# Cache loads of the last two steps on GpSimd's DMA queue, in a decode kernel whose order is computed by a scheduler

## The chip, the core and the metric

The kernel runs on one core of a Trainium2 chip. The metric is device time in microseconds (us) of one execution. The core has five instruction streams that matter here: TensorE (PE), VectorE (DVE), ScalarE (ACT), GpSimd (POOL) and SyncE (SP). Each runs its own instructions strictly in the order in which the program lists them. SP does nothing but issue DMA transfers; GpSimd computes and issues DMAs too. The transfers that SP issues go into one DMA queue (q1 in the profile), those of GpSimd into another (q0). Both queues are served by the same 16 DMA engines.

## What is computed

A forward pass and all its gradients, for two batch rows of one token each (decode), everything in bf16:

```python
xn  = layernorm(x)                         # x: [2, 1, 576]
q   = xn @ wq                              # 32 query heads of 128, 16 cache heads
p   = softmax(q . k_cache * 128**-0.5)     # k_cache, v_cache: [2, 16, 4096, 128]
out = x + (p @ v_cache) @ wo + ((xn @ w_gate) * (xn @ w_up)) @ w_down
# outputs: out, and the gradients for grad_out of
# x, k_cache, v_cache, wq, wo, w_gate, w_up, w_down
```

The caches hold 32 MB each, and their gradients have the same size. So 64 MB of cache are read and 64 MB of cache gradient are written; the weights (wq, wo, w_gate, w_up, w_down) add about 25 MB in each direction. The gradients are outer products: the gradient of V for a head is p (4096 long) times the incoming gradient (128 long), that of K is the score gradient times q.

## The kernel before

**Steps.** The work on the caches is cut into 16 steps (`NS`), numbered s = 0 to 15. A step handles two cache heads (l = 0, 1) of one batch row; two steps (the two batch rows) make a group, and there are 8 groups. In a step, t = 0 stands for K and t = 1 for V. Each (s, t, l) is one tile of 128 partitions x 8192 bytes, 1 MB, loaded whole by one DMA: 4 loads in a step, 64 in all. They are issued in `load_kv` (the DMA is on line 986).

**What a step does.** `turn` transposes each loaded tile on DVE in two halves (line 411). `softmax` multiplies the transposed K by the queries (`score`, 64 small matmuls, line 1096), takes the softmax and spreads the probabilities into the layout that the next matmuls want (`spread`, lines 1103 and 1104, through the tile `sp`, then a DVE transpose into `pp`). `dscore` does the same for V with the incoming gradient, and gets the score gradient, which it spreads through the same tile `sp` into `dd`. `contract` multiplies the untransposed tile by `pp` or `dd` (line 1272); only after that is the 1 MB buffer of the load free (`free_kv`). `outer` and `head_outer` make the gradient of the cache: matmuls against `BD`, a block-diagonal tile that GpSimd builds (line 1084, 4 in a group, one per step and t), two PSUM banks at a time, copied to a 1 MB buffer by ACT (line 415) or DVE (line 417), four copies for one buffer. The full buffer is stored by one DMA of SP (line 642, in `put`). There are 64 such stores of 1 MB.

**Weights.** Each group has a `group_front` (queries, loads of wq and wo) and a `group_back` (gradients of wq and wo). Nine blocks of the gated MLP (`mlp`) are sprinkled over the steps. The loads of wq, wo, w_gate and w_up and the stores of all weight gradients (0.5 and 0.56 MB, and tails of 64 KB) are issued by GpSimd; w_down is loaded by SP. After the last group, `final_out` and `final_dx` write out the two small results `out` and the gradient of x.

**Buffers.** Sixteen buffers of 1 MB (`big`) are shared by three users: loaded cache tiles (`kv`), transposed tiles (`X`) and stores being filled or in flight (`st`). `CAP` says how many each user may hold at once.

**Who sets the order.** The program has no order of its own. Every piece of work is a Python generator that yields requests (`ACQ` a buffer, `WAIT` for an event, occupy an engine for so long, issue a `DMA`), and the class `Order` runs them all in a simulated time before the chip sees anything. For each engine it takes, among the requests that can start within `SLACK` us of the earliest one, that with the lowest priority number, and the instructions are emitted in that order. Priorities are `PR[name] + STEP * s`, with corrections in `HEAD` for the first two steps and `TAIL` for the last two. `CAP`, `BIAS` (how readily a PSUM copy goes to DVE instead of ACT), `MLPD` (distance of MLP blocks, in cache loads) and `WO0` shift the order too. On the chip, semaphores guard every dependency: a wrong guess of the order costs waiting.

Two consequences matter. SP's list holds cache loads and cache stores mixed: a load stands behind every store that precedes it in the list, first on SP (which waits until that store's data is ready) and then in the DMA queue. And GpSimd's list holds `BD` builds, small copies and DMA issues mixed, with the same rule.

Of the kernel before, what the change touches and what calls it, by code (L numbers as in the profile page):

```python
# [95 lines left out]
class Order:  # L96

    HOP, TAIL, DRAIN = 0.07, 0.18, {"PE": 0.0, "ACT": 0.1, "DVE": 0.075, "POOL": 0.0}

# [84 lines left out]
    def run(self):  # L184
        while self.streams:
# [8 lines left out]
            if e is not None:  # L194
                t, _, s, e = min((c for c in cand if c[3] == e and c[0] <= t + SLACK[e]), key=lambda c: (c[1], c[0]))
            r = s.req
            value = None
            if r[0] in ("op", "any"):
                cost = r[2] if r[0] == "op" else next(c for x, c, _ in r[1] if x == e)
                quad = r[3] if len(r) > 3 else None  # L200
                if e == "PE":
                    end = t + cost + self.TAIL
                    if quad is not None and self.quad[:2] == (1 - quad, t):
                        cost, end = 0.02, max(t + self.TAIL, self.quad[2]) + 0.02
                    self.quad, self.kind = (quad, t + cost, end), r[6]
# [29 lines left out]
def PE(stream, issue=0.0, quad=None, kind="f"):  # L235
    return ("op", "PE", max(CLK * stream, issue) + 0.03, quad, stream, issue, kind)


def DVE(cost):
    return ("op", "DVE", cost)  # L240
# [10 lines left out]
def EV(cols):  # L251
    return ("any", [("ACT", 0.16 + cols * 0.00083, 0.0), ("DVE", 0.145 + cols * 0.00104, cols / 1024 * BIAS)])


def ACQ(tag):
    return ("acq", tag)


def REL(tag, i):
    return ("rel", tag, i)  # L260


def WAIT(*events):
    return ("wait", events)


def SET(event):
    return ("set", event)


def SPAWN(gen, prio):
    return ("spawn", gen, prio)


def PRIO(prio):
    return ("prio", prio)


def DMA(engine, cost, nbytes, row=8192):
    packet = 0.0375 * row + 9.0  # L280
    return ("dma", engine, cost, 0.08 + nbytes / 16e3 * packet / row, packet)
# [1 line left out]


NBIG, NGU, NWW, NBD = 16, 1, 5, 3
CAP = {"kv": 8, "X": 14, "st": 12}
MLP0, MLPD = 0, 7.5
KVSTORE = "SP"
WQ0, WO0 = 0, 0
LATENCY, DRY = {"SP": 0.5, "ACT": 0.5, "POOL": 0.57}, 0.4  # L290
CLK = 2.0
BIAS = 0.63
SLACK = {"PE": 0.09, "ACT": 0.09, "DVE": 0.4, "POOL": 17.41, "SP": 26.84}
STEP = 28.0
HEAD = {"turn0": 3.0, "turn1": -11.1, "att": -19.9, "dsc": -4.3, "con": -39.4, "conv": -28.9, "out1": 42.9, "out0": 22.1, "front": -45.5, "back": 29.8, "W1": 86.9, "BD1": -12.5, "BD0": -10.4, "load": -8.1}
TAIL = {"turn0": 28.4, "turn1": 45.6, "att": 15.9, "dsc": -167.2, "con": -11.9, "conv": -61.9, "out1": -25.1, "out0": 3.1, "front": 0.8, "back": -31.6, "BD1": -11.1, "BD0": -158.9, "load": -37.4}
PR = {"turn0": -37.7, "turn1": 50.3, "att": -846.2, "dsc": -882.4, "conv": 130.3, "con": -283.8, "out1": 415.4, "out0": 232.2,
      "front": 147.9, "back": -713.6, "W0": 247.3, "W1": 250.7, "BD1": 345.9, "BD0": -138.7, "mlp": -163.6, "wout": -835.0,
      "store": 1037.0, "load": -22.4, "wload": -455.4, "fin": 234.1, "const": 420.2, "mload": 222.9}


def pr(name, s):
    edge = {} if type(s) is not int else HEAD if s < 2 else TAIL if s > 13 else {}
    return STEP * s + PR[name] + edge.get(name, 0)


@with_exitstack
def kernel(
# [22 lines left out]
    nc = tc.nc  # L331
# [7 lines left out]
    G = 2  # L339
    GH = 2 * G  # L340
    NG = Hkv // G
    NS = NG * Bq
# [12 lines left out]
    const = ctx.enter_context(tc.tile_pool(name="const", bufs=1))  # L355
# [4 lines left out]
    def tiles(tag, n, shape, dtype=BF16):  # L360
        od.ring(tag, n)
        return [const.tile(list(shape), dtype, name=f"{tag}{i}") for i in range(n)]

    kv_t = X_t = st_t = tiles("big", NBIG, [P, NCH * Dh])
    od.share("big", CAP)
    Xt_t = tiles("Xt", 1, [P, FS])
# [46 lines left out]
    def cp(e, out, in_):  # L413
        if e == "ACT":
            nc.scalar.copy(out, in_)  # L415
        else:
            nc.vector.tensor_copy(out=out, in_=in_)  # L417
# [100 lines left out]
    def front():  # L518
# [57 lines left out]

        yield PRIO(PR["const"])
        yield WAIT(Econst)
# [50 lines left out]
    class Store:  # L629
# [3 lines left out]
        def done(self):  # L633
            self.n -= 1
            if self.n == 0:
                yield SPAWN(self.out(), self.prio + PR["store"])

# [45 lines left out]
    def rows_outer(lhs, dst, p, events=()):  # L683
        i = yield ACQ("st")
        st = st_t[i]
        src = st[:, 0:FC * D].rearrange("p (h n) -> p h n", h=FC)
        store = Store(FC, put("POOL", [(dst, src, 128 * FC * D * 2)], "st", i, events, 4608), p)
        for a in range(FC):
            yield SPAWN(unit(*rows_unit(a, lhs, st), store), p)
# [35 lines left out]
    def mlp(i, Lgu, Ld, gs_slot, wd_slot):  # L725
# [41 lines left out]
        E = [Event() for _ in range(4)]  # L767
        po = pr("mlp", (MLP0 + i * MLPD) / 4) + PR["wout"]
        yield SPAWN(rows_outer(lambda a: hb[32 * a:32 * a + 32, 0, :],
# [125 lines left out]
    def group_back(g):  # L895
# [15 lines left out]
        E = [Event() for _ in range(3)]  # L911
        po = pr("back", 2 * g) + PR["wout"]
        yield SPAWN(rows_outer(lambda a: R[32 * a:32 * a + 32, 0, :],
# [60 lines left out]
    views = [A.rearrange("b h (p c) d -> b h p (c d)", p=P) for A in (A_k_cache, A_v_cache)]  # L974
    oviews = [A.rearrange("b h (p c) d -> b h p (c d)", p=P) for A in (out_2, out_3)]

    def load_kv():
        n = 0
        for s in range(NS):
            g, b = divmod(s, Bq)  # L980
            yield PRIO(pr("load", s))
            for t in range(2):
                for l in range(G):
                    i = yield ACQ("kv")
                    yield DMA("SP", 0.36, 1 << 20)
                    nc.sync.dma_start(kv_t[i][:], views[t][b, G * g + l])
                    kvS[s][t][l] = i
                    yield ("lset", kvL[s][t][l])
                    yield SET(issued[n])
                    n += 1  # L990
# [99 lines left out]
    def score(t, s, sc, l):  # L1090
        X = X_t[xS[s][t][l]]
        W = W_t[t][wS[s][t]]
        for be in range(4):
            for c2 in range(2):
                for cq in range(4):
                    nc.tensor.matmul(  # L1096
                        sc[32 * cq:32 * cq + 32, :],
                        lhsT=view(W[:], 0, P, (be * G + l) * WW + 6 - 4 * c2 - 2 * l, [[1, 32]]),
                        rhs=view(X[:], 0, P, (2 * cq + c2) * Dh + 64 * (be // 2) + be % 2, [[8 * Dh, 4], [2, 32]]),
                        start=(l == 0 and be == 0 and c2 == 0), stop=(l == G - 1 and be == 3 and c2 == 1))  # L1100

    def spread(src, dst_ps):
        nc.tensor.matmul(dst_ps[:, 0:P], lhsT=identP[:], rhs=src[:], start=True, stop=True)
        nc.tensor.matmul(dst_ps[:, P:2 * P], lhsT=src[:], rhs=identP[:], start=True, stop=True)
# [100 lines left out]
    def dscore(s):  # L1205
        S = steps[s]
        yield WAIT(wE[s][1], S["sm"], *xE[s][1])
        k = yield ACQ("m")
        dp = m_t[k][:, 0:P]
        for l in range(G):  # L1210
            yield PE(0.427, 0.224, kind="c")
            score(1, s, dp, l)
            yield REL("X", xS[s][1][l])
        yield REL("W1", wS[s][1])
        c = ch_t[S["ch"]]
        yield DVE(0.35)
        nc.vector.tensor_tensor_reduce(
            out=c["ds"][:], in0=c["ex"][:], in1=dp, scale=1.0, scalar=0.0,
            op0=ALU.mult, op1=ALU.add, accum_out=c["cs"][:],
        )  # L1220
        m = yield ACQ("m")
        yield PE(0.0, 0.1)
        nc.tensor.matmul(m_t[m][:, 0:1], lhsT=G4[:].rearrange("p a m -> p (a m)"), rhs=c["cs"][:], start=True, stop=True)
        yield DVE(0.15)
        nc.vector.tensor_tensor(c["cr"][:], m_t[m][:, 0:1], c["rz"][:], ALU.mult)  # L1225
        yield REL("m", m)
        yield DVE(0.3)
        nc.vector.scalar_tensor_tensor(out=c["ds"][:], in0=dp, scalar=c["cr"][:], in1=c["pr"][:],
                                       op0=ALU.subtract, op1=ALU.mult)
        yield REL("m", k)  # L1230
        S["dd"] = yield ACQ("dd")
        m = yield ACQ("m")
        yield PE(0.107, 0.052)
        spread(c["ds"], m_t[m])
        e = yield EV(256)
        cp(e, c["sp"][:], m_t[m][:, 0:2 * P])
        yield REL("m", m)
        yield DVE(0.4)
        t32(dd_t[S["dd"]][:].rearrange("p t n -> p (t n)"), c["sp"][:])
        yield REL("ch", S["ch"])  # L1240
        yield SPAWN(outer(s, 0, "dd", S["dd"], dd_t[S["dd"]][:, 1]), pr("out0", s))
        S["ddT"] = dd_t[S["dd"]][:]
        yield SPAWN(contract(s, 0), pr("con", s))
# [80 lines left out]
    def final_out():  # L1324
        yield PRIO(PR["fin"])
        yield WAIT(Eprep, *acc_E)
# [104 lines left out]
```

## Time and profile before

| | |
|---|---|
| median of 6 runs | 483.54 us (482.64 to 486.23) |
| profiled execution | 483.57 us, of which the span of the profile is 481.8 us |
| DMA | 185.94 MB, mean 386 GB/s; q1 (SP) 139.61 MB, q0 (GpSimd) 45.38 MB |
| busy, share of the span | PE 77%, DVE 72%, ACT 72%, GpSimd 51% |

How to read it: the span runs from the first to the last instruction of the profiled execution; the other 1.8 us lie around it. The page divides the span into 40 slices of about 12 us and gives for each the busy tenths of every engine, the mean busy share of the 16 DMA engines, and the GB/s that they moved. A list of waits names, for each engine and line, what it waited for. SPq is SP's queue of DMA issues. For a DMA, the profile tells when it was issued and when its last byte had landed.

### The profile page before, as it was taken

The numbers are of one execution on the slowest core, as the hardware profiler recorded it, in microseconds if no ns is written. First come the engines' busy times: TensorE is split into PE (matmuls) and PEld (weight loads), VectorE is DVE, ScalarE is ACT, GpSimd is POOL, SyncE is SP. The second block draws the span as 40 slices with busy tenths as digits, with TensorE's granted clock in tenths as the row PEclk, the third lists the DMA queues.
The fourth block names the chain that finished last, engine by engine and source line by source line (L and its number), as shares of the span: only waits on it lengthen the run. The fifth ranks groups of instructions, "written<-read, shape, count | busy, mean of one in ns | idle before, by whom it ended". The sixth has DMA issues, their size and how long they took to land.

```text
span 481.8 us, 14592 instructions
## 1 busy us (share of the span) xinstructions
PE 369.4 (77%) x6122; PEld 210.3 (44%) x6122; DVE 348.1 (72%) x662; ACT 346.1 (72%) x525; POOL 244.5 (51%) x348
## 2 busy tenths in 40 slices
PE   0578779664788589859776888887798878788886
PEld 0444445433454253435543543644454344434334
DVE  6798655883979465679887886887687775779763
ACT  6078847564889378917978589777867965878992
POOL 6185702772559126536384665272573756155501
PEclk9986765566786655565787577656656665857775
DMA  8999999899889999999999999999999999999995
GB/s 305 387 407 383 404 405 387 304 356 417 325 312 381 395 419 421 411 408 396 367 384 361 419 363 420 402 412 409 424 413 398 411 422 417 409 409 420 373 378 201
DMA packets 33445, 185.94 MB, mean 386 GB/s; under 512 B 5034, under 2 KB 5170, under 8 KB 16994
## 3 DMA queue, kind: packets, MB, share of 16 engines
q1 hardware_dynamic: 19866, 139.61, 72.1%
q0 software_dynamic: 13504, 45.38, 25.1%
q8 instruction: 48, 0.79, 0.6%
q14 instruction: 19, 0.16, 0.1%
q10 hardware_dynamic: 8, 0.00, 0.0%
HBM read 92.48 MB, written 92.48 MB: 384 GB/s over the span
## 4 chain that ended last, share of the span: by engine, by line
DMA 47%; PE 18%; ACT 10%; DVE 10%; POOL 8%; issue 7%; SPq 0%; POOLq 0%; DVEq 0%; ACTq 0%
DMA out_dram<-big 26%; DMA gu<-in_B_w_up_dram 10%; ACT big L415 8%; DVE big L411 6%; DMA ww<-in_B_w_down_dram 5%; DMA ww<-in_A_wq_dram 5%; PE ps_o L1118 4%; POOL BD L1084 3%; PE ps_m L1096 3%; PE ps_m L1272 2%; PE ps_m L756 2%; POOL gu L1019 1%; POOL out_dram L642 1%; DVE big L417 1%; PE ps_o L662 1%
## 5 line engine op out<-in xcount | busy, mean ns | idle before, releaser
L415 ACT CAST big<-ps_o 128x1024 bf16<-128x1024 f32 (+1 forms) x325 | 288.5, 964 | 41.3 <-PE ps_o L1118 26.8
L411 DVE STREAM_TRANSPOSE big<-big 128x1024 f32<-128x1024 f32 x128 | 153.2, 1220 | 17.1 <-DMA out_dram<-big 12.4
L1084 POOL TENSOR_TENSOR BD<-vr,mask 128x2048 bf16<-128x2048 bf16 x32 | 115.3, 3602 | 64.8 <-DVE vr L417 43.7
L417 DVE CAST big<-ps_o 128x1024 bf16<-128x1024 f32 (+1 forms) x51 | 56.6, 1112 | 15.6 <-PE ps_o L1118 5.9
L1096 PE MATMUL ps_m<-big,W 128*32 128x128 bf16 x2048 | 60.2, 285 | 8.1 <-DVE big L411 5.5
L1096 PEld LDWEIGHTS <-W 128*32 128x32 bf16 x2048 | 48.4, 127 | 27.6 <-issue 22.9
L1118 PE MATMUL ps_o<-BD,pp 32*128 32x512 bf16 x256 | 51.1, 519 | 11.5 <-ACT big L415 6.9
L1118 PE MATMUL ps_o<-BD,dd 32*128 32x512 bf16 x256 | 47.7, 509 | 10.4 <-ACT big L415 8.6
L642 POOL DMA_DIRECT2D out_dram<-big x43 | 33.4, 777 | 35.3 <-ACT big L415 16.1
L411 DVE STREAM_TRANSPOSE big<-ww 128x1152 f32<-128x1152 f32 x25 | 34.1, 1364 | 9.0 <-DMA out_dram<-big 7.3
L613 POOL COPY wt<-wm 64x128 bf16<-64x128 bf16 (+1 forms) x34 | 8.9, 262 | 60.6 <-DVE wm L607 56.6
L1061 POOL COPY W<-rep 32x16 bf16<-32x16 bf16 x128 | 24.7, 193 | 20.0 <-DVE rep L863 14.8
L1272 PE MATMUL ps_m<-big,pp 128*32 128x512 bf16 x256 | 30.1, 578 | 3.0 <-DVE cr L1225 1.8
L1272 PE MATMUL ps_m<-big,dd 128*32 128x512 bf16 x256 | 28.4, 535 | 3.5 <-ACT big L415 1.8
L1118 PEld LDWEIGHTS <-pp 32*128 32x128 bf16 x256 | 11.1, 99 | 31.8 <-issue 28.4
L411 DVE STREAM_TRANSPOSE big<-gu 128x1024 f32<-128x1024 f32 x18 | 21.5, 1225 | 1.9 <-DMA out_dram<-big 1.3
L1118 PEld LDWEIGHTS <-dd 32*128 32x128 bf16 x256 | 11.6, 99 | 24.8 <-issue 14.0
L642 POOL DMA_DIRECT2D out_dram<-tl x26 | 14.5, 560 | 12.2 <-ACT tl L415 11.6
L738 PE MATMUL ps_m<-gu,xs 128*32 128x128 bf16 x360 | 11.8, 296 | 11.5 <-DMA gu<-in_B_w_up_dram 8.9
L890 POOL COPY qr<-qd 128x256 bf16<-128x256 bf16 x8 | 3.2, 396 | 32.4 <-ACT qd L888 32.4
L879 PE MATMUL ps_m<-big,Wdy 128*128 128x128 bf16 x144 | 14.3, 276 | 4.3 <-ACT big L415 2.5
L415 ACT CAST osb<-ps_m 128x512 bf16<-128x512 f32 x16 | 9.6, 603 | 10.6 <-PE ps_m L1272 10.3
(207 smaller groups left out, 568.5 us busy)
## 6 DMA issues: line engine op xcount, KB each, us to landing
out_dram<-big SPq DMA_DIRECT2D x64, 1024.0 KB, 13.6
big<-in_A_k_cache_dram SPq DMA_DIRECT2D x32, 1024.0 KB, 12.7
big<-in_A_v_cache_dram SPq DMA_DIRECT2D x32, 1024.0 KB, 18.5
out_dram<-big POOLq DMA_DIRECT2D x26, 512.0 KB, 11.7
out_dram<-big POOLq DMA_DIRECT2D x17, 576.0 KB, 9.2
ww<-in_B_w_down_dram SPq DMA_DIRECT2D x9, 576.0 KB, 26.9
ww<-in_A_wo_dram POOLq DMA_DIRECT2D x8, 576.0 KB, 14.8
gu<-in_B_w_gate_dram POOLq DMA_DIRECT2D x9, 512.0 KB, 13.2
```

Of the source, the lines that this page charges most:

```text
L411: nc.vector.transpose(out, in_)
L415: nc.scalar.copy(out, in_)
L417: nc.vector.tensor_copy(out=out, in_=in_)
L642: (nc.gpsimd if engine == "POOL" else nc.sync).dma_start(dst, src)
L738: nc.tensor.matmul(ug[32 * a:32 * a + 32, 1 - w, :], lhsT=xs[:, dc if dc < 4 else 4 + w, :], rhs=gu[:, FS * k + P * a:FS * k + P * (a + 1) ...
L756: nc.tensor.matmul(dh, lhsT=Wdy[:, e, 2 * k:2 * k + P], rhs=view(X[:], 0, P, 64 * k + e, [[D, FC], [2, 32]]), start=(k == 0 and e == 0), s ...
L879: nc.tensor.matmul(dp, lhsT=Wdy[:, e, 2 * k:2 * k + P], rhs=view(X[:], 0, P, 64 * k + e, [[D, GH], [2, 32]]), start=(k == 0 and e == 0), s ...
L1061: nc.gpsimd.tensor_copy(view(W_t[t][w][:], 32 * a, 32, 6 + 8 * a, [[G * WW, 4], [WW, G], [1, 2]]), view(rep_t[grp[g]["qs"]][:], 32 * a, 32 ...
L1084: nc.gpsimd.tensor_tensor(BD_t[i][:], view(vr_t[v][:], 0, P, 0, [[0, 16], [1, Dh]]), view(mask16[:], 0, P, 0, [[1, 16], [0, Dh]]), ALU.mult)
L1096: nc.tensor.matmul(sc[32 * cq:32 * cq + 32, :], lhsT=view(W[:], 0, P, (be * G + l) * WW + 6 - 4 * c2 - 2 * l, [[1, 32]]), rhs=view(X[:], 0 ...
L1118: nc.tensor.matmul(o[:, k, :], lhsT=pr2[32 * c4:32 * c4 + 32, :], rhs=BD[32 * c4:32 * c4 + 32, 8 * l + 4 * h2:8 * l + 4 * h2 + 4, :], star ...
L1272: nc.tensor.matmul(ct[32 * j:32 * j + 32, :], lhsT=view(rT, 0, P, 4 * c + 2 * l, [[1, 32]]), rhs=kv_t[kvS[s][t][l]][:, Dh * c:Dh * (c + 4) ...
```

## The change

Three things change.

1. The 8 cache loads of the last two steps (s = 14 and 15, `late = s > NS - 3`) are issued by GpSimd instead of SP. The other 56 stay on SP. All cache stores stay on SP.
2. `dscore` waits for the event `spread` of its step before it spreads the score gradient. The event says that `softmax` of the step is done with the tile `sp`. This is a wait of the scheduler, and settles the order in which the two uses of `sp` are emitted.
3. The constants of the scheduler are new: the caps of `X` (14 to 9) and `st` (12 to 6), `BIAS`, `MLPD`, `WO0`, the slacks, and all priorities. The same instructions are made; their order on all five engines is another, and a PSUM copy can move between ACT and DVE.

```diff
-CAP = {"kv": 8, "X": 14, "st": 12}
-MLP0, MLPD = 0, 7.5
+CAP = {"kv": 8, "X": 9, "st": 6}
+MLP0, MLPD = 0, 7.56
 KVSTORE = "SP"
-WQ0, WO0 = 0, 0
+WQ0, WO0 = 0, 1
-BIAS = 0.63
-SLACK = {"PE": 0.09, "ACT": 0.09, "DVE": 0.4, "POOL": 17.41, "SP": 26.84}
+BIAS = 0.52
+SLACK = {"PE": 0.07, "ACT": 0.1, "DVE": 0.43, "POOL": 13.32, "SP": 24.35}
...
 (HEAD, TAIL and PR: all priorities are new, for example)
-"att": -846.2, "dsc": -882.4, "out1": 415.4, "out0": 232.2, "back": -713.6, "wout": -835.0, "store": 1037.0, "load": -22.4
+"att": -799.2, "dsc": -846.3, "out1": 779.6, "out0": 361.8, "back": -19.7,  "wout": -269.6, "store": 569.2,  "load": 67.8
@@ load_kv
                     i = yield ACQ("kv")
-                    yield DMA("SP", 0.36, 1 << 20)
-                    nc.sync.dma_start(kv_t[i][:], views[t][b, G * g + l])
+                    late = s > NS - 3
+                    yield DMA("POOL" if late else "SP", 0.78 if late else 0.36, 1 << 20)
+                    (nc.gpsimd if late else nc.sync).dma_start(kv_t[i][:], views[t][b, G * g + l])
@@ dscore
         yield REL("m", k)
+        yield WAIT(S["spread"])
         S["dd"] = yield ACQ("dd")
```

More of the change, by code (lines that the diff above doesn't have):

```diff
@@ L285 @@
 NBIG, NGU, NWW, NBD = 16, 1, 5, 3
-CAP = {"kv": 8, "X": 14, "st": 12}
-MLP0, MLPD = 0, 7.5
+CAP = {"kv": 8, "X": 9, "st": 6}
+MLP0, MLPD = 0, 7.56
 KVSTORE = "SP"
-WQ0, WO0 = 0, 0
+WQ0, WO0 = 0, 1
 LATENCY, DRY = {"SP": 0.5, "ACT": 0.5, "POOL": 0.57}, 0.4
 CLK = 2.0
-BIAS = 0.63
-SLACK = {"PE": 0.09, "ACT": 0.09, "DVE": 0.4, "POOL": 17.41, "SP": 26.84}
+BIAS = 0.52
+SLACK = {"PE": 0.07, "ACT": 0.1, "DVE": 0.43, "POOL": 13.32, "SP": 24.35}
 STEP = 28.0
[L295 to L299, printed above, removed]
+HEAD = {"turn0": 7.6, "turn1": 9.2, "att": -312.9, "dsc": -65.5, "con": -9.2, "conv": 27.5, "out1": 18.0, "out0": -270.5, "back": -57.7, "W0": -22.4, "W1": -29.5, "BD1": -2.1, "BD0": -24.2, "load": -9.0}
+TAIL = {"turn0": -63.8, "turn1": 1.3, "att": -112.4, "dsc": 46.2, "con": 16.3, "out1": -30.9, "back": 0.9, "W0": 4.9, "W1": 6.5, "BD1": -11.1}
+PR = {"turn0": -44.7, "turn1": -110.2, "att": -799.2, "dsc": -846.3, "conv": 0.0, "con": -188.2, "out1": 779.6, "out0": 361.8,
+      "front": 276.6, "back": -19.7, "W0": 149.5, "W1": 411.7, "BD1": 372.0, "BD0": -108.4, "mlp": -119.5, "wout": -269.6,
+      "store": 569.2, "load": 67.8, "wload": -287.1, "fin": 95.4, "const": 15.9, "mload": 40.3}
 def pr(name, s):
```

## The prediction

> **What bounds the kernel now.** I read the page's row of slices first, to see which resource is full and where it is not.
>
> ```profile
> ACT  6078847564889378917978589777867965878992
> DMA  8999999899889999999999999999999999999995
> GB/s 305 387 407 383 404 405 387 304 356 417 325 312 381 395 419 421 411 408 396 367 384 361 419 363 420 402 412 409 424 413 398 411 422 417 409 409 420 373 378 201
> ```
>
> The DMA engines are full nearly everywhere, so the bytes set the time. Full means about 415 GB/s. Against that, the first 14 slices (12.05 us each) lose 18.7 us, the next 23 lose 7.9, the last three (373, 378, 201) lose 8.5. The last three lie behind the last cache load, where the moved loads act, so I cut them finer.
>
> ```profile
> core 0: us, PE busy (x) PEld busy (x) DVE busy (x) ACT busy (x) POOL busy (x), PEclk, DMA share, GB/s
> 372.00:444.00 72.00, 58.20 (x941) 30.45 (x936) 54.07 (x96) 55.83 (x83) 40.92 (x48) 0.65 1.02 415
> 444.00:468.00 24.00, 20.28 (x337) 10.09 (x338) 18.42 (x33) 23.53 (x34) 7.55 (x8) 0.82 0.97 390
> 468.00:481.80 13.80, 9.56 (x88) 5.65 (x86) 4.25 (x14) 4.73 (x8) 2.56 (x5) 0.50 0.53 201
> ```
>
> Three regimes follow each other. Up to 444 us DMA is the bound, and ACT idles 16 of 72 us. From 444 to 468 no load is left and ACT is busy 23.53 of 24 us: copies from PSUM are the bound. After 468 a chain of small steps ends the kernel with the DMA half empty. ACT idles while DMA is full, and is full once DMA is not; so I ask how late the last data came. First SP's cache loads from 370 us on (durations are of the issue, in ns), then GpSimd's stores from 372 on:
>
> ```profile
> L986 SPq DMA_DIRECT2D big<-in_A_k_cache_dram x4: 339/339/357, 375.8 to 407.7; - x4
> L986 SPq DMA_DIRECT2D big<-in_A_v_cache_dram x4: 327/334/339, 389.7 to 414.9; - x4
> ...
> DMA to landing us min/median/max: 25.1/26.8/27.6
> ```
>
> ```profile
> L642 POOL DMA_DIRECT2D out_dram<-big x10: 752/769/792, 399.3 to 471.1; - x10
> ...
> DMA to landing us min/median/max: 5.9/10.8/14.5
> ```
>
> These are exactly the eight loads that move. A load waits 26.8 us in SP's queue behind stores; a GpSimd transfer of half the size lands in 10.8. The last V tile, issued at 414.9, is there only at 441.
>
> **The change part by part.**
>
> *Eight loads leave SP.* SP saves 8 x 0.34 = 2.7 us of issue. SP has no other work, and its late stores wait for ACT's copies: worth 0.
>
> *They join GpSimd's queue.* No 1 MB load on GpSimd is in the trace; its issue lies between the 0.56 us of a 64 KB tail and the 0.79 of a w_gate load. I take the 0.77 of its 0.5 MB stores: 6.2 us. On SP the loads also stood waiting, mostly for buffers (370 to 420 us):
>
> ```profile
> SPq L986 <- PE ps_m L1272: 8.1, 2, 6.7
> SPq L986 <- DMA out_dram<-big: 3.9, 2, 2.1
> SPq L986 <- DVE big L417: 3.5, 1, 3.5
> SPq L986 <- DMA big<-in_A_v_cache_dram: 3.5, 1, 3.5
> ```
>
> With the smaller ones that is 22.0 us, and it now blocks GpSimd. Wait and issue need 28.2 us; GpSimd idles 72 - 40.9 = 31.1 between 372 and 444. It fits, by a margin of 3: I cost it at nothing, and at 5 us if the cover fails (first rival). Passed in the queue are the last MLP block's weights and the last group's wq and wo. Behind a 1 MB transfer at half of 415 GB/s each lands up to 5 us later; its gradient stores were issued from 451 to 455, over 20 us before the end, so 0 to 5, taken as 0.
>
> *What the loads gain.* Here the Trainium skill speaks against the change: "DMA: Bandwidth & Descriptors", section "Issuing engines are not separate DMA queues", says that DMAs from several engines run on the same 16 DMA engines and interleave, so that a second issuing engine saves only issue time. By that the sum is 2.7 us of SP time off the path: 483.6, no change. The two landing rows say more: the same engines, but 26.8 against 10.8 us, since a transfer waits for its own queue's backlog. Bandwidth is not gained, the order of landing is. I go by the rows. Twice the size at half rate adds 0.5 MB / 207 GB/s = 2.5 us: about 13.4 us to land, 13 sooner. The last four tiles then are there at about 420 to 428 instead of 434 to 441. If the loads queue up behind each other (5 us each) the last one gains only some 5; both ends stay in the range.
>
> *What the engines make of it.* Work can then move into this idle time:
>
> ```profile
> 426.00:432.00 6.00, 4.95 (x95) 2.32 (x87) 3.88 (x4) 4.33 (x7) 3.08 (x1) 0.50 1.02 415
> 432.00:438.00 6.00, 4.37 (x60) 1.78 (x63) 5.70 (x11) 5.16 (x7) 4.24 (x2) 0.78 1.02 424
> 438.00:444.00 6.00, 5.52 (x97) 2.95 (x95) 4.98 (x11) 4.12 (x7) 2.97 (x1) 0.63 1.01 426
> ```
>
> ACT idles 18 - 13.6 = 4.4 us there and DVE 18 - 14.6 = 3.4: 7.8 us of copies and transposes, taken out of a later stretch that two engines share, shorten it by 3.9. The upper bound is DMA: after 444 there remain 24 x 390 + 13.8 x 201 = 12.1 MB, 29.2 us at 415, and the last small store takes 2.2 us from its issue; that ends at 475.4, 6.4 us early. Nothing comes off if the closing chain does not start earlier. I take 3.9.
>
> *The stores that are overtaken* land later, up to 2.6 us for each load ahead of them, and hold their buffers; see the second rival.
>
> *The wait for `spread`.* It adds no instruction. In the last step the probabilities are spread at 447.8 and the score gradient at 452.6, so the order it asks for is there already. Bounds 0 to 1 us a step, if the new order had wanted otherwise; taken 0.
>
> *The remade order.* The trace cannot show it. Its price is bounded by the dry stretches of before: the slices at 304, 325 and 312 each lose about 3 us, so that an order with two fewer gains 6 and one with two more loses 6. Nothing decides the sign; 0, and plus or minus 6 in the range.
>
> Sum: -3.9 us. The profiled execution took 483.57 us (span 481.8 and 1.8 around it), practically the median of 483.54, so **479.7 us**.
>
> **The rivals.**
>
> *GpSimd becomes the late engine (slower).* Its list is in order. A load that waits 6.7 us for a contract stands in front of `BD` builds (3.6 us each), and the gradient copies of the last two steps wait for those. For it: the margin is only 3 us, and PE already waited for `BD` 4 times, 3.1 us in all. Against it: GpSimd was idle before its own builds for up to 5.3 us, waiting for `vr`, and a load can stand there. It decides when a slot wait of over 5.3 us precedes a build. Two such blocks, 6.7 each, less 4.2 recovered in the idle ahead of the last build: about 9, of which the ACT-bound stretch hides some 4. 483.6 + 5 = 488.6.
>
> *Six store buffers are too few (slower).* From 372 to 444 SP issued 11 stores that took about 22 us to land, GpSimd 5 that took 12: (242 + 60) / 72 = 4.2 in flight, and one or two being filled. That is just under the new cap of 6, and overtaken stores hold longer. Each store held back when DMA runs dry costs 2.6 us; two give 489. With the remade order opening dry stretches, up to 491.
>
> *Nothing to see.* The earlier loads only swap places with stores, and the closing chain or a dry stretch takes the rest: 481.5 to 485.5.
>
> **How the numbers follow.** A measurement of this kernel can tell about 0.5% from no change: below 481.1 is faster, above 486.0 slower. The last data coming earlier: 0.40, around 479.7 (475 to 481). The same with dry stretches closed: 0.05, 470 to 475. Nothing to see: 0.19. GpSimd late: 0.15, around 488.6. Buffers and dry stretches: 0.21, 487 to 493. So faster 0.45, same 0.19, slower 0.36. The likeliest case's own range is 475 to 481; holding 8 in 10 over both signs needs 474 to 490.5.
>
> **What would show it.** Right: the eight loads appear on POOL, landing in 8 to 16 us; the last V tile lands before 432; ACT idles less before 444; the GB/s of the last slice is well over 201. Wrong: GpSimd idle before a load for over 5 us with PE waiting for `BD` behind it (first rival); ACT or PE idle on DMA out_dram in the middle of the kernel, or new slices near 310 GB/s (second); loads landing in 20 us or more (the landing term).

## The result, and the profile after

The changed kernel takes 489.14 us (median of 16 runs, 485.87 to 493.44); the kernel before took 484.36 (median of 37). The ratio is 1.0100, with a 95% interval of 1.0075 to 1.0125. The change is slower by 4.8 us, where I had forecast faster by 4. The profiled execution took 487.94 us, its span is 486.2.

First the rows of slices again, each slice now 12.16 us:

```profile
ACT  6069955588962687976658983789795873948984
DMA  8999999999999989999999999999999999998685
GB/s 307 389 408 352 401 389 423 357 379 390 423 409 385 372 326 335 392 418 404 414 399 416 358 396 421 407 408 421 400 400 420 416 418 399 399 417 351 219 362 197
```

Up to slice 36 nothing is lost: the dry stretches lie elsewhere than before, and there are not more of them. Then comes 351, 219, 362. Added up over time, the bytes moved by 440 us are 173.0 MB against 172.0 before, so the new order is 2.4 us ahead (1 MB at 415 GB/s). Twenty microseconds later it is 3.3 us behind. This is that stretch, before, after, and in a variant that is told below (`a_tails`), in this order (busy us with the number of instructions for each engine, then TensorE clock, DMA share, GB/s):

```profile
440.00:460.00 20.00, 17.60 (x312) 9.07 (x300) 15.83 (x32) 17.94 (x29) 8.51 (x9) 0.77 0.97 386
```

```profile
440.00:460.00 20.00, 18.25 (x307) 10.74 (x295) 17.94 (x31) 17.39 (x29) 10.47 (x10) 0.67 0.71 271
```

```profile
440.00:460.00 20.00, 18.11 (x339) 10.36 (x338) 17.67 (x31) 17.18 (x29) 9.64 (x7) 0.76 0.83 324
```

271 instead of 386 GB/s for 20 us is 2.3 MB, or 5.5 us of transfer. The engines are busy there; DMA has too little to do, since results that it should store come late: SP issues no store between 428.6 and 439.7 us, where before it issued two. So the cause lies earlier. In the finer table of after it is the stretch just ahead of it:

```profile
432.00:444.00 12.00, 8.21 (x129) 4.21 (x128) 4.55 (x8) 7.18 (x10) 8.00 (x9) 0.50 0.91 372
```

Here DVE works 4.55 of 12 us; before it was 10.68. The granted TensorE clock is 0.50 here and stays there until 446 us; before, it was 0.71 in this stretch. How much of the loss lies in that was not tested. What PE, ACT and DVE wait for is in their timelines (start, duration, engine, line, operation, and in brackets the idle time before it and what ended it):

```profile
428.01 0.23 PE L1077 MATMUL ps_m<-ident,qr 128*128 128x128 bf16 x1
435.10 0.61 PE L1119 MATMUL ps_o<-BD,pp 32*128 32x512 bf16 x4 [6.86 <-POOL BD L1085]
```

```profile
435.74 3.76 ACT L415 CAST big<-ps_o 128x1024 bf16<-128x1024 f32 x4 [6.27 <-PE ps_o L1119]
```

```profile
438.44 1.22 DVE L417 CAST big<-ps_o 128x1024 bf16<-128x1024 f32 x1 [7.69 <-PE ps_o L1119]
```

All three stand still for 6 to 8 us behind one `BD` build of GpSimd. GpSimd's own timeline tells why that build is late:

```profile
404.08 0.76 POOL L1020 DMA_DIRECT2D gu<-in_B_w_gate_dram  x1
404.83 0.54 POOL L1023 DMA_DIRECT2D gu<-in_B_w_gate_dram  x1
...
407.58 0.78 POOL L1020 DMA_DIRECT2D gu<-in_B_w_up_dram  x1 [2.21 <-DMA out_dram<-big]
...
411.06 0.54 POOL L1023 DMA_DIRECT2D gu<-in_B_w_up_dram  x1 [2.70 <-DMA out_dram<-big]
...
415.45 0.56 POOL L987 DMA_DIRECT2D big<-in_A_k_cache_dram  x1 [3.85 <-PE ps_o L1119]
...
420.12 0.54 POOL L987 DMA_DIRECT2D big<-in_A_v_cache_dram  x1 [2.72 <-PE ps_o L662]
...
423.76 0.53 POOL L987 DMA_DIRECT2D big<-in_A_v_cache_dram  x1 [3.10 <-PE ps_o L1119]
...
428.61 0.77 POOL L642 DMA_DIRECT2D out_dram<-big  x1 [3.78 <-ACT big L415]
...
431.43 3.61 POOL L1085 TENSOR_TENSOR BD<-vr,mask 128x2048 bf16<-128x2048 bf16 x1
```

From 407.6 to 431.4 us GpSimd is busy for 6.9 us and waits before seven DMA issues for 18.8 in all. The brackets name different releasers for these waits: PE, ACT, a store. Two of them name a store for a *load of weights*, which has no use for that store. That is the clue. Every DMA signals its end on a semaphore of its queue, and the trace shows that each queue uses eight of them in turn, GpSimd's being 108 to 115. The ninth DMA therefore signals on the semaphore of the first. Set beside each other, worked out from the trace's issues and landings:

```
issue on GpSimd, us        semaphore   the eighth DMA before it    landed, us
407.58  w_up load          108         store of 392.01             407.30
411.06  w_up tail          109         store of 393.16             410.77
415.45  K load             110         store of 397.55             414.92
420.12  V load             111         V load of 400.72            419.49
423.76  V load             112         V load of 401.27            423.21
428.61  gradient store     113         K load of 403.56            428.02
430.08  gradient store     114         w_gate load of 404.08       429.50
```

Seven issues in a row come 0.3 to 0.6 us after the landing of the eighth DMA before them. In this program a queue has at most eight DMAs outstanding, and an issuing engine stops its whole list to keep to it. Before, GpSimd met this limit not once after 365 us. SP met it ten times from 380 to 423: there no computation stands behind the issues, and what the held loads and stores cost was not measured.

### The profile page after: what moved, and what is told of

It reads as the page before. It is cut to its first block, busy times and chain, and to the rows that moved or that the text cites. A ratio compares the mean times of both kernels' runs of the same rounds, so it can differ in the third digit from the quotient of the medians.

```text
span 486.2 us, 14587 instructions
## 1 busy us (share of the span) xinstructions
PE 371.7 (76%) x6122; PEld 211.2 (43%) x6122; DVE 350.8 (72%) x656; ACT 345.4 (71%) x531; POOL 248.9 (51%) x356
## 5 line engine op out<-in xcount | busy, mean ns | idle before, releaser
L417 DVE CAST big<-ps_o 128x1024 bf16<-128x1024 f32 (+1 forms) x53 | 60.7, 1147 | 17.5 <-PE ps_o L1119 11.9
L1119 PE MATMUL ps_o<-BD,pp 32*128 32x512 bf16 x256 | 54.8, 544 | 23.5 <-POOL BD L1085 12.5
L1097 PEld LDWEIGHTS <-W 128*32 128x32 bf16 x2048 | 46.9, 124 | 26.3 <-issue 23.1
L1119 PE MATMUL ps_o<-BD,dd 32*128 32x512 bf16 x256 | 45.9, 509 | 6.6 <-ACT big L415 5.1
L1274 PE MATMUL ps_m<-big,pp 128*32 128x512 bf16 x256 | 31.8, 600 | 2.7 <-DVE accx L824 1.4
L1119 PEld LDWEIGHTS <-dd 32*128 32x128 bf16 x256 | 10.7, 97 | 28.2 <-issue 21.8
L620 PE MATMUL ps_m<-big,wm 128*32 128x128 bf16 x416 | 14.2, 299 | 7.3 <-DVE big L411 6.2
L662 PEld LDWEIGHTS <-xnr 32*128 32x128 bf16 x416 | 14.9, 110 | 8.6 <-issue 7.5
L1284 ACT ACTIVATE osb<-ps_m 128x512 bf16<-128x512 f32 x16 | 9.6, 602 | 12.0 <-PE ps_m L1274 12.0
L662 PE MATMUL ps_o<-hb,xnr 32*128 32x128 bf16 x288 | 15.2, 250 | 3.3 <-ACT big L415 2.0
```

What stands on the lines that cost most here:

```text
L620: nc.tensor.matmul(dp[32 * q:32 * q + 32, 0:P], lhsT=view(Wm[:], 0, P, 8 * pos(q, s), [[1, 32]]), rhs=view(X, 0, P, xoff(q, s), [[xstep, 4 ...
L662: nc.tensor.matmul(o[:, aa, dc * P:(dc + 1) * P], lhsT=xnr[32 * a:32 * a + 32, dc * P:(dc + 1) * P], rhs=rhs(a), start=True, stop=True)
L1097: nc.tensor.matmul(sc[32 * cq:32 * cq + 32, :], lhsT=view(W[:], 0, P, (be * G + l) * WW + 6 - 4 * c2 - 2 * l, [[1, 32]]), rhs=view(X[:], 0 ...
L1119: nc.tensor.matmul(o[:, k, :], lhsT=pr2[32 * c4:32 * c4 + 32, :], rhs=BD[32 * c4:32 * c4 + 32, 8 * l + 4 * h2:8 * l + 4 * h2 + 4, :], star ...
L1274: nc.tensor.matmul(ct[32 * j:32 * j + 32, :], lhsT=view(rT, 0, P, 4 * c + 2 * l, [[1, 32]]), rhs=kv_t[kvS[s][t][l]][:, Dh * c:Dh * (c + 4) ...
L1284: nc.scalar.activation(ob, cs, AF.Copy, scale=SCALE)
```

## The experiments

The theories, as the expectations name them: **Q**, the queue of the eight loads makes the difference; **O**, the remade order does; **R**, GpSimd stops at eight outstanding DMAs; **B**, the bytes ahead in GpSimd's queue delay what it builds; **W**, the last group's wq comes late behind the loads. Ratios are to the kernel before, with 95% intervals.

### Queue and order taken apart

`a_sp` has the order of after on PE, DVE and ACT; SP issues the eight loads.

```diff
-(nc.gpsimd if late else nc.sync).dma_start(kv_t[i][:], ...)
+nc.sync.dma_start(kv_t[i][:], ...)
```

> The order of the changed kernel on PE, DVE and ACT instruction for instruction; only the eight late loads are issued by SP again, at the same places of the order. Theory Q (the queue: the loads block GpSimd's list and crowd its DMA queue, so that BD tiles come late and the last step's data too): the stretch 440 to 460, which lost 6 us of DMA against before, is repaired, and the 2.5 us of lead that the remade order had at 440 stays: 480 to 483 us, ratio to before 0.99 to 1.00. Theory O (the remade order itself is worse at its end, whatever queue the loads use): 487 to 490, like the changed kernel.

Measured: 490.13 us, 1.0106 (1.0078 to 1.0134).

`b_pool` has the order of before; GpSimd issues the eight loads, and the scheduler does not know it.

```diff
-nc.sync.dma_start(kv_t[i][:], ...)
+(nc.gpsimd if s > NS - 3 else nc.sync).dma_start(kv_t[i][:], ...)
```

> The order of the kernel before on PE, DVE and ACT instruction for instruction; only the eight loads of the last two steps are issued by GpSimd at the same places of the order. Theory Q: GpSimd waits for buffers in front of BD builds, 487 to 493 us. Theory O: the move alone does no harm, 481 to 485 us, and if the landing row of the prediction was right, the loads land in 8 to 16 us and the time is 480 or less.

Measured: 497.86 us, 1.0265 (1.0212 to 1.0317).

`a_nolate` has the new constants with the loads left on SP, and the order is worked out for that.

```diff
-late = s > NS - 3
+late = False
```

> The constants of the changed kernel, but the scheduler is told that all loads are issued by SP, and computes its order anew. Theory Q: 480 to 484 us. Theory O: the constants were fitted to the other queue, so that this order is no better than the changed kernel: 487 to 492.

Measured: 481.84 us, 0.9944 (0.9917 to 0.9971).

`b_late` is the code of after with the old constants.

> The constants of the kernel before, with the eight loads on GpSimd told to the scheduler, and the wait for spread. Theory Q: 486 to 492 us, since the loads still stand in GpSimd's list. Theory O: about 484, as before, within 3 us.

Measured: 502.85 us, 1.0343 (1.0292 to 1.0393).

The new constants with all loads on SP gain 0.56%. The loads on GpSimd lose wherever they are tried: 2.65 points in the order of before, 3.4 with the old constants and an order worked out for them (more than either theory had forecast), 1.6 from `a_nolate` to after. But the fixed order of after is no better with the loads back on SP. In that trace (`a_sp`), among the waits from 380 us on (engine, tile and line, what ended the wait: us in all, times, longest):

```profile
DVE big L411 <- DMA out_dram<-big: 7.4, 2, 5.7
...
PEld L620 <- DVE big L411: 6.4, 1, 6.4
```

DVE waits for a store to release a buffer for the transposed wq, and PE waits for that wq. That store is issued at 403.6 us, behind three of the loads in SP's queue, and lands at 427.4, after 23.7 us; in after, where the loads are in the other queue, the same store takes 11.7 us (405.7 to 417.4). The limit has no part in it: SP meets it only from 407.5 on. That is another stall of nearly the same size. So "O alone" cannot be read from `a_sp`: an order and the queue that it was made for go together.

### The limit, tested in the order of after

`a_tails` leaves the eight loads on GpSimd and moves to SP the small DMAs of the last stretch, 64 KB each: the last group's wq tail, the two tails of the last MLP block and the late gradient tails. They are nine (the expectation says seven).

```diff
-(nc.gpsimd if engine == "POOL" else nc.sync).dma_start(dst, src)
+(nc.gpsimd if engine == "POOL" and (tag != "tl" or od.free["POOL"] < 365) else nc.sync).dma_start(dst, src)
...
-(nc.gpsimd if i else nc.sync).dma_start(ww_t[w][:, 4 * FS:WB],
+(nc.gpsimd if 0 < i < NG - 1 else nc.sync).dma_start(ww_t[w][:, 4 * FS:WB],
...
-nc.gpsimd.dma_start(gu[64 * w:64 * w + 64, 8 * FS:9 * FS], ...)
+(nc.sync if i == NFS - 1 else nc.gpsimd).dma_start(gu[64 * w:64 * w + 64, 8 * FS:9 * FS], ...)
```

> The changed kernel with the order of PE, DVE and ACT as it is; the eight loads stay on GpSimd, but the 64 KB transfers of the last stretch (tails of gradient stores, of the last MLP block's and the last group's weight loads) are issued by SP at the same places of the order. They carry hardly any bytes. Theory R (GpSimd may have only eight DMAs outstanding; from 407 to 430 us each of its issues waited for the landing of the eighth before it, and the BD builds behind them came 12 us late): fewer DMAs in GpSimd's list let it run ahead, BD builds come some 3 to 6 us earlier, 484 to 487 us. Theory B (the loads are late because GpSimd's queue has too many bytes before them): 488 to 490, as the changed kernel.

Measured: 482.23 us, 0.9975 (0.9954 to 0.9996). `a_split` goes the other way: each of the eight loads as two DMAs of half the size, so that the same bytes take eight more places.

```diff
-(nc.gpsimd if late else nc.sync).dma_start(kv_t[i][:], ...)
+for r in ((slice(0, 64), slice(64, P)) if late else (slice(0, P),)):
+    (nc.gpsimd if late else nc.sync).dma_start(kv_t[i][r, :], ...)
```

> The changed kernel with each of the eight late loads issued as two DMAs of 64 partitions, same bytes, same queue, same order of everything else. Theory R: the places among the eight outstanding DMAs are used up twice as fast, GpSimd stalls earlier and longer, 492 to 498 us. Theory B: as the changed kernel, at most 1 us more, 489 to 490.

Measured: 500.22 us, 1.0345 (1.031 to 1.0379). GpSimd's timeline in `a_tails` and then in `a_split`, and PE's in `a_split`:

```profile
404.26 0.76 POOL L1020 DMA_DIRECT2D gu<-in_B_w_gate_dram  x1
405.01 0.76 POOL L1020 DMA_DIRECT2D gu<-in_B_w_up_dram  x1
405.77 0.55 POOL L987 DMA_DIRECT2D big<-in_A_k_cache_dram  x1
...
412.89 1.07 POOL L987 DMA_DIRECT2D big<-in_A_v_cache_dram  x2 [1.55 <-DVE big L417]
...
422.76 3.62 POOL L1085 TENSOR_TENSOR BD<-vr,mask 128x2048 bf16<-128x2048 bf16 x1
```

```profile
420.94 0.79 POOL L1020 DMA_DIRECT2D gu<-in_B_w_up_dram  x1 [3.08 <-DMA big<-in_A_v_cache_dram]
424.25 0.53 POOL L1023 DMA_DIRECT2D gu<-in_B_w_up_dram  x1 [2.53 <-DMA big<-in_A_v_cache_dram]
...
442.81 3.61 POOL L1085 TENSOR_TENSOR BD<-vr,mask 128x2048 bf16<-128x2048 bf16 x1
```

```profile
446.48 0.62 PE L1119 MATMUL ps_o<-BD,pp 32*128 32x512 bf16 x4 [4.52 <-POOL BD L1085]
```

Without the small transfers the issues go out one behind the other and `BD` starts at 422.8 instead of 431.4; PE no longer waits for it. With the loads halved, `BD` starts at 442.8, after 15 issues that waited at the limit, and the time rises. But `a_tails` takes away three things at once: places, bytes, and GpSimd's time for the issues. Two kernels put one back each. `a_places` issues, where each moved transfer stood, a DMA of 512 bytes into a tile that nothing uses; `a_busy` makes two memsets there, together about as long as an issue.

```diff
 a_places, behind each transfer moved to SP:
+nc.gpsimd.dma_start(scr_t[next(scr_n)][:], A_wq[512:576, 0:4])
 a_busy, in the same places:
+[nc.gpsimd.memset(scr_t[:], 0.0) for _ in range(2)]
```

> As the changed kernel with its 64 KB transfers of the last stretch moved to SP (482 us), but where each of them stood in GpSimd's list there is now a DMA of 512 bytes into an unused tile. GpSimd's issue time and the places among its outstanding DMAs are those of the changed kernel again, the bytes are not. Theory R (places): back to 486 to 490 us. If it was the bytes, or the sooner landing on SP, that helped: 481 to 483.5.

Measured: 484.2 us, 1.0004 (0.9988 to 1.002).

> The same, with two short memsets of GpSimd (about 0.5 us together) in place of each 64 KB transfer: GpSimd's time is spent, no place among the outstanding DMAs is taken. Theory R: 481 to 484 us, as without them. If the time of GpSimd's issues was what counted: 486 to 490.

Measured: 482.7 us, 0.9976 (0.9951 to 1.0001). The starts of the same `BD` build, in `a_busy` and in `a_places`:

```profile
421.46 3.60 POOL L1085 TENSOR_TENSOR BD<-vr,mask 128x2048 bf16<-128x2048 bf16 x1
```

```profile
427.78 3.61 POOL L1085 TENSOR_TENSOR BD<-vr,mask 128x2048 bf16<-128x2048 bf16 x1
```

All five kernels have one order and the eight loads on GpSimd:

| kernel | issues on GpSimd that waited at the limit after 365 us | `BD` starts, us | time, us |
|---|---|---|---|
| `a_busy` | 0 | 421.5 | 482.7 |
| `a_tails` | 0 | 422.8 | 482.2 |
| `a_places` | 7 | 427.8 | 484.2 |
| after | 7 | 431.4 | 489.1 |
| `a_split` | 15 | 442.8 | 500.2 |

Issue time costs nothing that shows: 482.7 against 482.2 us. Nine places with next to no bytes bring the limit back, seven times, start `BD` 6.3 us later than in `a_busy` and cost 1.5 us, less than R had forecast (486 to 490 us). The rest of the way to after, 0.96 points or 4.6 us, comes with the 0.6 MB that these transfers carry in the same queue. At half of 415 GB/s they delay the landings behind them by some 2.8 us (an estimate). The traces agree: the store that the first of the seven issues waits for goes out at 391.7 us in `a_places` and at 392.0 in after, and lands at 404.8 and at 407.3; `BD` comes another 3.6 us later. The same places cost more when what fills them lands later.

From `a_places` on, the time moves with the build: `BD` starts 3.6 us later in after and another 11.4 later in `a_split`, and the profiled executions (484.1, 487.9 and 499.2 us) are 3.8 and 11.3 us longer. Between `a_busy` and `a_tails`, whose builds are 1.3 us apart, it does not.

So R holds in this order. That B acts through it fits the landings but is in part argued, since the bytes and the places in SP's queue that the nine transfers had taken changed together; how much the bytes would cost with no limit at all was not tried, nor was an order planned with the limit in the scheduler's model.

### K and V on different queues

`a_v` issues the late K tiles on GpSimd and the V tiles on SP; `a_tails_v` moves the small transfers too.

```diff
-(nc.gpsimd if late else nc.sync).dma_start(kv_t[i][:], ...)
+(nc.gpsimd if late and t == 0 else nc.sync).dma_start(kv_t[i][:], ...)
```

> The changed kernel's order; K loads of the last two steps on GpSimd, V loads on SP, 64 KB transfers on GpSimd. Theory R: four DMAs fewer among GpSimd's eight, so BD builds come as early as with the 64 KB transfers moved: 482 to 485 us. Without R, since all eight loads on SP gave 490 and all eight on GpSimd 489: 489 to 490.

Measured: 491.05 us, 1.0145 (1.0112 to 1.0179).

> As the last, and the seven 64 KB transfers on SP too. With the limit out of the way already, this asks whether earlier landing gains what the prediction said: the last V tile, which landed at 442 us with only the 64 KB transfers moved, is expected at 428 to 434. If earlier data shortens the end: 478 to 480.5 us. If the end is bound by the copies and the closing chain whatever the loads do: 481.5 to 483.5.

Measured: 488.72 us, 1.012 (1.0081 to 1.0158). Both are misses. R had forecast 482 to 485 us for `a_v`; and in `a_tails_v`, where no issue of GpSimd waits at the limit, the last V tile lands at 435.6 us, 6.5 sooner than in `a_tails`, and the kernel is 1.45 points slower. What both show is the wait of `a_sp`, for the transposed wq. DVE in `a_v` and in `a_tails_v`:

```profile
426.61 1.38 DVE L411 STREAM_TRANSPOSE big<-ww 128x1152 f32<-128x1152 f32 x1 [4.86 <-DMA out_dram<-big]
```

```profile
428.33 1.38 DVE L411 STREAM_TRANSPOSE big<-ww 128x1152 f32<-128x1152 f32 x1 [5.64 <-DMA out_dram<-big]
```

The stores that end these waits are issued at 401.9 and 404.4 us, behind two V loads on SP, and land at 426.6 and 428.3. SP meets the limit not once in `a_v` and nine times in `a_tails_v`, so this wait does not need it. What one queue is spared, the other gets.

### The other orders: a miss

If R were all, the same cure would work in the orders of before and of `a_nolate`. `n_pool` is `a_nolate` with the edit of `b_pool`; `b_pool6` moves only the last six loads; `b_pool_tails` and `n_pool_tails` are `b_pool` and `n_pool` with the small transfers on SP; `b_pool6_tails` is `b_pool6` with the tails of the last MLP block and of the gradients on SP, and wq and wo left where they were.

> The order computed with the new constants and all loads on SP (481.8 us), with only the issue of the eight late loads moved to GpSimd. If the loss belongs to GpSimd's queue and not to one particular order: 488 to 496 us, as the same move did to the kernel before. If the move is harmless in a better order: 480 to 484.

Measured: 497.14 us, 1.0278 (1.0238 to 1.0318).

> The order of the kernel before with only the last six loads on GpSimd; the two K loads of step 14 stay on SP, so that nothing new stands ahead of the last group's wq and wo in GpSimd's queue. Theory W (with all eight moved, the 13 us of loss came from wq landing 8 us later, for which PE waited 9 us, so that the whole last group began late): 484 to 489 us. Without that mechanism (the loss comes from the last six loads and the wait for outstanding DMAs): 493 to 498.

Measured: 496.85 us, 1.0272 (1.0236 to 1.0308).

> The order of the kernel before, all eight late loads issued by GpSimd, and the seven 64 KB transfers of the last stretch issued by SP. Theory R (the limit of eight outstanding DMAs is what makes the move costly in any order): GpSimd no longer waits for landings, most of the 13 us is gone, 484 to 489 us. If in this order the loss is bytes (w_gate and w_up of the last MLP block stand behind 1 MB loads, and PE waited 6.6 us for them with six loads moved): 493 to 498.

Measured: 499.54 us, 1.0331 (1.0291 to 1.0372).

> The order of the new constants with all loads planned on SP, the eight late loads issued by GpSimd, the seven 64 KB transfers by SP. Theory R: 484 to 489 us, against 497 with the 64 KB transfers on GpSimd. By bytes: 494 to 498.

Measured: 498.87 us, 1.0333 (1.0297 to 1.0368).

> The order of the kernel before, the last six cache loads on GpSimd, the 64 KB transfers of gradient tails and of the last MLP block on SP, the last group's wq and wo where they were. Neither wq (which was late with all eight loads moved) nor the limit of eight (met four times with six moved) then applies. If these two together made the loss of 13 us: 484 to 489 us. If w_gate and w_up standing behind 1 MB loads are enough: 494 to 498.

Measured: 494.82 us, 1.0226 (1.0205 to 1.0246).

In both `..._pool_tails` kernels the limit is not met once, and they are not faster. The waits that stand out, in `b_pool`, `b_pool6` and `b_pool6_tails` in turn:

```profile
PE ps_m L846 <- DMA ww<-in_A_wq_dram: 8.9, 1, 8.9
```

```profile
PE ps_m L738 <- DMA gu<-in_B_w_up_dram: 6.6, 1, 6.6
```

```profile
DVE big L411 <- DMA out_dram<-big: 11.6, 3, 7.2
```

In `b_pool` wq lands at 397.2 us instead of 389.5, behind two K loads of 1 MB. With these two left on SP (`b_pool6`) it lands at 390.0, and the time is 496.85 instead of 497.86, so W alone is not the cause either: a wait for w_up has taken its place. Without that one, DVE waits for stores. Each remedy uncovers another late transfer. That the move costs 11 to 19 us in these orders, each against its own time with all loads on SP, is shown; which of their many changed landings sets it is left open.

## Why the prediction was wrong

**What bounds the kernel** was read rightly for before. In after, DMA is full only up to 438 us, and the time was lost where I had looked for the gain.

**"They join GpSimd's queue", cost 0, failed.** I compared two sums, 28.2 us of waiting and issue against 31.1 of idleness, and called it cover. But it was not the sum that counted: seven waits stood one after another in front of one `BD` build, which started at 431.4 us instead of 422.8 (`a_tails`), and that cost 1.25 points, or 6.0 us. Nor were they waits for buffers. They were for room among the eight outstanding DMAs, and SP's list of waits had shown that already: 3.5 us for the landing of another V tile, 3.9 for stores, in front of *loads*. The 3.5 put down to DVE belong there too, for of the two loads that waited so long (issued at 389.68 and 414.89) each followed the landing of the V tile eight DMAs before it (389.61 and 414.82). So 10.9 of the 22.0 us that I had booked as waiting mostly for buffers were this limit. The issue term was a little too large: 0.53 to 0.61 us for a load, not 0.77, and `a_busy` shows no cost of issue time here.

**"What the loads gain", 13 us, failed.** After:

```profile
L987 POOL DMA_DIRECT2D big<-in_A_k_cache_dram x4: 531/566/613, 376.0 to 415.5; - x4
L987 POOL DMA_DIRECT2D big<-in_A_v_cache_dram x4: 528/545/559, 400.7 to 423.8; - x4
...
DMA to landing us min/median/max: 9.8/20.2/24.5
```

The loads take 20.2 us to land, not 13.4, and the last is issued at 423.8 instead of 414.9. It lands at 444.1, where before it was 440.9 and I had said 428. The row of 10.8 us belonged to a queue that, from 400 to 430 us, had 4.9 transfers in flight on average, beside 7.6 in SP's. With 8 MB of loads moved it was the deep one, with 7.7, and SP's had 2.3. I carried a queue's delay over without the load that I was adding to it. The Trainium skill's section "Issuing engines are not separate DMA queues" in "DMA: Bandwidth & Descriptors", which I set aside for that row, has another issuer save nothing but issue time, and the end of the kernel agrees: even in `a_tails`, with no limit in the way, the loads take 18.4 us, the last V lands at 442.1, no sooner than before, and the time is no better than that of `a_nolate`, with all loads on SP.

**"What the engines make of it", -3.9,** fell with it: ACT and DVE did not fill their idle time, they got 6.3 and 7.7 us more of it at one place.

**The `spread` wait and SP's relief**, 0 each: no wait for either shows among those from 370 us on; neither was run alone.

**The remade order**, 0 plus or minus 6: its size was inside the bounds. Planned for SP it gains 0.56%, and with GpSimd's loads freed of the limit 0.25%. In after it hides part of the loss: 6.0 us of stall less 1.2 is the +4.8.

**The rivals.** The first, GpSimd as the late engine, had the right engine, the right line and 488.6 us. Its wait was another, though: not a buffer held by a contract, but the landing of the eighth DMA before; so that its number came close is luck. The sign that I had named for it, over 5 us of idleness before one load, did not come either: the longest was 3.85. Its counter-argument, that a load can stand in GpSimd's idle time, failed because these waits come one after another, each ended by a landing, and add up ahead of the build. The second rival did not come: at most 7 stores are in flight, as before, and the slices in the middle are no drier.

Of the kernels here `a_nolate` has the lowest ratio, and is faster than before and after: the new constants, with the loads left on SP. Its interval overlaps that of `a_tails`.

## What to carry to other kernels

Before moving DMAs to an engine that computes, count how many it will have outstanding and how long each takes to land under the *new* load: here, past eight, every issue waited for a landing, and all computation behind it waited too. A small transfer takes a place as a large one does, so put small ones where no computation stands behind them. And look at what else is in the queue that the moved DMAs leave or join: here, stores behind the loads on SP cost as much. An order written out for one choice of queues is tried again, not kept, when the queue is changed.

## What was not expected of the hardware

- Each queue of this program has at most eight DMAs outstanding; seven issues of GpSimd came 0.3 to 0.6 us after the landing of the eighth before. The profile names for such a wait whatever finished at about that time, also PE and ACT.
- A DMA of 512 bytes takes a place for as long as the ones ahead of it in the queue are under way: one issued at 404.5 us landed at 426.2, and nine of them moved a `BD` build from 421.5 to 427.8 us.
- A load of 1 MB takes GpSimd 0.55 us to issue, less than its 0.5 MB stores (0.77).
